# Features out of PSUM: one VectorE product per tile in place of two ScalarE copies, in a top-k attention with capacity-dropped experts

## The chip, the cores and the metric

One core of a Trainium2 chip runs the whole program. The metric is device time in microseconds (us) of one execution. The engines are called as in the profile: PE is TensorE (matmuls and transposes; PEld its weight loads), DVE is VectorE, ACT is ScalarE, POOL is GpSimd, SP is SyncE, whose queue issues most of the DMAs.

## What is computed

Eight sequences of 576 tokens with 8 heads of size 64 go through an attention that keeps, in each row, the scores not below the 32nd largest. The result, as 4608 tokens of 512 features, goes to a mixture of 8 experts, where each expert takes at most 80 of the tokens that choose it.

```python
scores = scale * np.matmul(q, k.transpose(0, 1, 3, 2))
kth = np.partition(scores, -top_k, axis=-1)[..., -top_k:-top_k + 1]
scores = np.where(scores >= kth, scores, -1000000000.0)
attn = np.exp(scores - np.max(scores, axis=-1, keepdims=True))
attn = attn / (np.sum(attn, axis=-1, keepdims=True) + 1e-09)
x = np.matmul(attn, v)                       # heads side by side: 4608 x 512
...
logits = x @ w_gate                          # one expert per token, 80 at most per expert
h = np.maximum(x[tok_idx] @ w1[e], 0.0)
out[tok_idx] = gate_w[tok_idx, None] * (h @ w2[e])
```

The change is in the division by the sum: the features `x` of a tile are what the product with `v` left in PSUM, times the reciprocal of the row's sum.

## The kernel before

**Tiles.** Attention works on pairs of heads: 8 sequences with 4 pairs each make 32 head pairs `n`. The 576 rows of a pair are cut into four full tiles of 128 rows (t = 0 to 3), each with both heads, and one tail tile of 64 rows (t = 4), in which the two heads lie on partitions 0 to 63 and 64 to 127. A unit is one head of one full tile, or the tail tile: 9 units a pair, 288 in all. `run` makes one step per unit, and the instructions of a step belong to several units at different stages.

**Stages of a unit.** `front` (PE, L226) makes the scores in the PSUM tile `sp`; ACT copies them, scaled, to `s` (L233). DVE takes the eight largest of each of six pieces (`cand`, L241), and from these searches the 24th largest in `search` (L252, L260). ACT then counts how many scores lie above it with a Sign pass (L257), POOL multiplies scores and signs to `y` (L263), DVE takes the eight next from `y` (L265), and a small DVE operation, the pick (L268), writes the threshold. `below` makes the mask from it: for odd units on ACT (L277), for even ones on POOL (L279). `turn_w` transposes scores and masks together on PE into PSUM (L315, L320; tiles `ab` and `cc`), ACT takes the exponential into `wT` (L322, L324), and `back` multiplies with `v` on PE (L335). Its result for head h stands in `cc` from column 256 + 65 h on: 64 features and, as 65th column, the sum of the weights.

**The division.** `over` lets DVE take the reciprocals of the sums, for both heads at once, into `z_all` (L347; the letter "z" in the order). `divide` then brings the features to `xn` in SBUF with one ACT copy per head (L358), whose scale is the column of reciprocals: 2 copies of 128x64 for a full tile, 2 of 64x64 for the tail tile. That frees `cc`, of which there are two.

**Behind it.** When a pair is complete, `norm` stores `xn` to the DRAM tensor `xd` with two DMAs on SP (L367, L369), transposes it on PE (L201), copies it on ACT (`xT`, L375), multiplies it with the gate weights (L380), and ACT copies the logits out (L387); for all but the first pair of a sequence DVE adds them up (L391). After every second sequence, `gates` works on the logits of two sequences together (L402 to L425). `turn` transposes the q and k of the next pair (L201) into `sp`, and ACT copies them as `both` (L214).

**What sets the order.** Everything in `run` is under a manual schedule: each engine executes its instructions in the order in which `step` issues them. In a step, a string of letters gives the order on DVE first; behind it come `turn_w`, `divide`, `front`, `back` and the `norm` pieces. "G" is one L241, "a" the last of these and the first L252, "b", "c", "d", "e", "y", "g" and "h" move the `search` of a unit one to four steps back on by one instruction each; "z" is the reciprocal, "m" and "M" are the masks. Because a pair has nine steps, its tiles end on odd steps in one pair and on even steps in the next, so that what surrounds "z" repeats every 18 steps.

```python
for c in "GybGcGdGeGGzag" if i % 2 else "GGbghHmMyGcGdGeGza":
...
if whole(i - 4):
    self.turn_w(*units[i - 4][:2])
for u in done:
    self.divide(*u)
```

After attention, `route` and `finish` choose the tokens and run the experts; the change doesn't touch them. A second, slower form of the whole program (`batch`, with `lean`) follows behind a condition that doesn't hold for these inputs.

Of the kernel before, what the change touches and what calls it, by code (L numbers as in the profile page):

```python
# [14 lines left out]
Act = mybir.ActivationFunctionType  # L15
Alu = mybir.AluOpType
# [11 lines left out]
def kernel(  # L28
# [11 lines left out]
    nc = tc.nc  # L40
    B, H, S, D = q.shape
# [7 lines left out]
    scale = 1.0 / math.sqrt(D)  # L49
    P = 128  # L50
    HP = H // 2
    NP = B * HP
    NF = S // P
    TL = S - NF * P
# [94 lines left out]
    class Attention:  # L149
# [199 lines left out]
        def divide(self, n, t):  # L349
            if t == 0:  # L350
                self.xn[n] = self.rows.tile([P, NK, 2, D], F32, name="xn", tag="xn")
            cc = self.w.pop((n, t))
            for h in range(2):
                if t < NF:
                    p, o, j, m = slice(0, P), 2 * P + h * (D + 1), h, P
                else:
                    p, o, j, m = slice(TL * h, TL * h + TL), 2 * P, 0, TL
                nc.scalar.activation(self.xn[n][:m, t, h, :], cc[p, o : o + D], Act.Copy, scale=self.z[p, n % NP, t, j : j + 1])  # L358

        def norm(self, n, b, hp, bi, nb, cs=range(NK)):  # L360

# [65 lines left out]
        def run(self, slow):  # L427

            units = []
            for n in range(NP):  # L430
                for t in range(NF):
                    units += [(n, t, 0), (n, t, 1)]
                units.append((n, NF, 2))
            self.odd = set(range(1, NU, 2))
            first, second = {}, {}
            later = []
            due = []
            drawn = []
            ready = {}

            def whole(i):

                return 0 <= i < NU and units[i][2] > 0

            def step(i, last):
                if 0 <= i < NU:
                    n, t, h = units[i]
                    if t == 2 and h == 1 and n + 2 < NP:
                        self.load(n + 2, *divmod(n + 2, HP))
                    if t in (1, 3) and h == 0 and slow and n:  # L450
                        slow.pop(0)()
                    if t == 0 and h == 0 and n + 1 < NP:
                        due.append(n + 1)
                    first[i] = self.parts(i)


                back = dict(a=0, b=1, c=1, d=1, e=1, y=2, g=3, h=4, m=4, H=3, M=3)
                for c in "GybGcGdGeGGzag" if i % 2 else "GGbghHmMyGcGdGeGza":
                    if c == "G":
                        if 0 <= i < NU:  # L460
                            next(first[i])
                    elif c == "a":
                        if 0 <= i < NU:
                            next(first[i], None)
                            second[i] = self.search(i)
                            next(second[i])
                    elif c == "z":
                        for u in drawn:
                            self.over(*u)
                    elif c in "mM":  # L470
                        if 0 <= i - back[c] < NU:
                            self.below(i - back[c])
                    elif i - back[c] in second:
                        next(second[i - back[c]])
                done = list(drawn)
                drawn.clear()

                def back():
                    if whole(i - 5):
                        self.back(*units[i - 5][:2])  # L480
                        drawn.append(units[i - 5][:2])


                rest = whole(i - 4) and units[i - 4][2] == 2
                if rest:
                    back()
                if whole(i - 4):
                    self.turn_w(*units[i - 4][:2])
                for u in done:
                    self.divide(*u)  # L490

                ends = [(n, range(NK) if n < NP - 1 else range(NF) if t < NF else range(NF, NK))
                        for n, t in done if t == NF or (n == NP - 1 and t == NF - 1)]

                f = i + 4 if i not in (0, 1) else i + 3
                busy = 0 <= f < NU and units[f][2] != 1
                if busy:
                    self.front(*units[f][:2])
                if not rest:
                    back()  # L500
                if due and not busy and i > 0:
                    self.turn(due.pop())
                    busy = True
                for g in list(later):
                    if ready[g] and busy and not last:
                        continue
                    busy = busy or ready[g] == 1
                    ready[g] = next(g, None)
                    if ready[g] is None:
                        later.remove(g)  # L510
                for n, cs in ends:
                    b, hp = divmod(n, HP)
                    later.append(self.norm(n, b, hp, b % 2, 2, cs))
                    ready[later[-1]] = 0

            with tc.manual_schedule():
                self.load(0, 0, 0)
                self.load(1, *divmod(1, HP))
                nc.sync.dma_start(wg, moe_w_gate.rearrange("(c p) e -> p c e", p=P))
                self.turn(0)  # L520
                i = -4
                while i < NU + 6 or later:
                    step(i, i >= NU + 5)
                    i += 1
            assert not slow and not due
# [389 lines left out]
```

## Time and profile before

Three runs took 994.33, 994.34 and 996.04 us; the median is 994.34. The profiled execution took 994.13 us, of which its span, from the first to the last instruction, is 992.4 us. The mean granted TensorE clock is 0.983.

| what | from the profile |
|---|---|
| profiled execution, its span | 994.13 us, 992.4 us |
| L358, the copies to `xn` on ACT | 320, busy 86.6 us, 324 ns (128x64) and 305 ns (64x64) |
| L347, the reciprocals on DVE | 160, busy 24.6 us, 152 ns (128x2) and 159 ns (128x1) |
| L241, the largest of six pieces, DVE | 1728, busy 400.6 us, 246 ns |
| L265, the largest of `y`, DVE | 288, busy 216.4 us, 752 ns; DVE idle before it 45.8 us, for POOL's `y` |
| L263, `y` on POOL | 288, busy 365.3 us, 1280 ns; POOL idle before it 65.9 us, for ACT's sign |
| L279, masks on POOL | 144, busy 247.9 us, 1722 ns; POOL idle before it 178.3 us, mostly for the pick |
| L335, product with `v`, PE | 5760, busy 205.2 us; PE idle before it 42.7 us, for `wT` |
| L391, sum of the logits on DVE, 128x40 | 23, 199 ns in the mean |

A group's line in the profile gives the number of instructions, how long their engine was busy with them, the mean duration of one, and how long the engine had stood idle just before them, with what ended the wait. Durations on one engine overlap: the next instruction often starts before the last one has ended, so the time between two starts, the step, is the price of an instruction in a full queue, and it is shorter than its duration. "L358 ACT xn<-cc,z_all" reads: line 358, on ACT, writes `xn` from `cc` and `z_all`.

### The profile page before, as it was taken

The page shows a single profiled execution, that of the slowest core. Times are in us where ns is not written, and L with a number is a line of the kernel's source. Part 1 is how long each engine was busy: PE and PEld are TensorE (multiplying, and loading weights), DVE is VectorE, ACT ScalarE, POOL GpSimd, SP SyncE. Part 2 cuts the span into 40 slices and gives each one's busy share as a digit, 9 for nine tenths or more (in the row PEclk, how much of TensorE's full clock was granted, in tenths as well). Part 3 has the DMA queues.
Part 4 walks back from the last instruction along what each step waited for, and adds up shares of the span by engine and source line. Part 5 has one row for each costly group of instructions (what it writes and reads, how often), then busy time and mean ns, then how long its engine had stood idle before and what let it go on. Part 6 is the DMA issues. An engine that isn't in the chain of part 4 may idle for free.

```text
span 992.4 us, 35679 instructions
## 1 busy us (share of the span) xinstructions
PE 881.3 (89%) x13368; PEld 710.3 (72%) x13368; DVE 804.6 (81%) x4928; ACT 798.2 (80%) x1652; POOL 627.3 (63%) x474
## 2 busy tenths in 40 slices
PE   5899999999989999999899999999899998689996
PEld 3677777777767777777677777777677776578896
DVE  5798989898989898999989898989898989471110
ACT  3899999999989999999899999999899999501110
POOL 3677767676767777777677676766677777402111
PEclk9999999999999999999999999999999999979999
DMA  3445453333323233333111122222222200084921
GB/s 72 102 123 133 126 135 91 92 92 92 93 76 77 75 87 86 88 90 92 46 41 44 44 50 50 51 50 49 49 50 50 50 13 14 16 339 147 368 85 29
DMA packets 167797, 85.76 MB, mean 86 GB/s; under 512 B 117696, under 2 KB 154560, under 8 KB 167616
## 3 DMA queue, kind: packets, MB, share of 16 engines
q1 hardware_dynamic: 166592, 80.78, 29.1%
q0 software_dynamic: 1024, 2.62, 0.9%
q8 instruction: 107, 1.75, 0.7%
q14 instruction: 74, 0.61, 0.2%
HBM read 63.19 MB, written 20.19 MB: 84 GB/s over the span
## 4 chain that ended last, share of the span: by engine, by line
DVE 46%; PE 26%; ACT 15%; POOL 7%; issue 5%; DMA 1%; POOLq 0%; SPq 0%; DVEq 0%; ACTq 0%
DVE cand L241 15%; DVE w L265 11%; DVE cand L260 6%; PE cc L335 5%; DVE top L252 5%; ACT sign L257 5%; POOL y L263 5%; PE sp L226 4%; PE yp L799 4%; DVE pick L268 3%; ACT wT L324 3%; ACT mask L277 3%; PE sp L201 2%; DVE w L252 2%; POOL mask L279 2%
## 5 line engine op out<-in xcount | busy, mean ns | idle before, releaser
L241 DVE MAX8 cand<-s 128x8 f32<-128x96 f32 x1728 | 400.6, 246 | 9.0 <-ACT s L233 8.8
L263 POOL TENSOR_TENSOR y<-s,sign 128x576 f32<-128x576 f32 x288 | 365.3, 1280 | 65.9 <-ACT sign L257 65.9
L279 POOL TENSOR_SCALAR mask<-s,thr_all 128x576 bf16<-128x576 f32 x144 | 247.9, 1722 | 178.3 <-DVE pick L268 175.4
L335 PEld LDWEIGHTS cc<-vb,wT 128*64 128x64 f32 x5760 | 182.8, 139 | 113.6 <-ACT wT L324 100.1
L265 DVE MAX8 w<-y 128x8 f32<-128x576 f32 x288 | 216.4, 752 | 45.8 <-POOL y L263 45.8
L335 PE MATMUL cc<-vb,wT 128*64 128x65 f32 x5760 | 205.2, 226 | 42.7 <-ACT wT L324 42.7
L257 ACT ACTIVATE sign<-s,w 128x576 bf16<-128x576 f32 x288 | 225.2, 782 | 7.1 <-POOL y L263 3.0
L226 PE MATMUL sp<-both 64*128 64x288 f32 (+1 forms) x1280 | 203.2, 437 | 17.5 <-ACT part L387 9.5
L233 ACT ACTIVATE s<-sp 128x1152 f32<-128x1152 f32 (+1 forms) x161 | 167.4, 1040 | 12.2 <-PE sp L226 9.9
L315 PE MATMUL ab<-ident,s 128*128 128x128 f32 x1148 | 176.2, 283 | 0.0
L324 ACT ACTIVATE wT<-ab 128x1024 f32<-128x1024 f32 (+1 forms) x159 | 149.1, 937 | 0.0
L226 PEld LDWEIGHTS sp<-both 64*128 64x128 f32 (+1 forms) x1280 | 106.1, 180 | 56.4 <-ACT part L387 11.4
L315 PEld LDWEIGHTS ab<-ident,s 128*128 128x128 f32 x1148 | 127.9, 142 | 11.6 <-issue 0.9
L252 DVE MAX8 top<-cand 128x8 f32<-128x48 f32 x576 | 116.0, 201 | 4.5
L277 ACT ACTIVATE mask<-s,thr_all 128x576 bf16<-128x576 f32 x144 | 112.4, 781 | 6.9 <-DVE pick L268 6.5
L320 PEld LDWEIGHTS <-mask 128*128 128x128 bf16 x1440 | 94.2, 98 | 31.9 <-POOL mask L279 29.2
L260 DVE MATCH_REPLACE8 cand<-top,cand 128x48 f32<-128x48 f32 x576 | 110.9, 193 | 0.0
L358 ACT ACTIVATE xn<-cc,z_all 128x64 f32<-128x64 f32 (+1 forms) x320 | 86.6, 320 | 1.2 <-DVE z_all L347 0.8
L315 PE MATMUL cc<-ident,s 128*128 128x128 f32 x288 | 79.1, 275 | 0.0
L322 ACT ACTIVATE wT<-cc 128x256 f32<-128x256 f32 (+1 forms) x160 | 56.9, 356 | 16.8 <-PE cc L320 15.5
L268 DVE SCALAR_TENSOR_TENSOR pick<-past,cnt,w 128x9 f32<-128x9 f32 x288 | 60.3, 223 | 0.3 <-ACT xn L358 0.3
L257 ACT ACTIVATION_READ_ACCUMULATOR sign<-s,w 128x1 f32 x288 | 58.7, 204 | 0.0
(187 smaller groups left out, 909.4 us busy)
## 6 DMA issues: line engine op xcount, KB each, us to landing
w<-in_moe_w_dram SPq DMA_DIRECT2D x10, 2048.0 KB, 11.6
w<-in_moe_w_dram SPq DMA_DIRECT2D x24, 512.0 KB, 4.6
out_dram<-zero SPq DMA_DIRECT2D x9, 1024.0 KB, 6.5
qn<-in_q_dram SPq DMA_DIRECT2D x64, 128.0 KB, 2.5
kn<-in_k_dram SPq DMA_DIRECT2D x64, 128.0 KB, 2.5
vb<-in_v_dram SPq DMA_DIRECT2D x64, 128.0 KB, 2.7
xd<-xn SPq DMA_DIRECT2D x32, 256.0 KB, 3.8
qn<-in_q_dram SPq DMA_DIRECT2D x32, 32.0 KB, 2.3
```

The source lines that it names most:

```text
L226: nc.tensor.matmul(o, lhsT=qT[d, t * P : t * P + m], rhs=kT[d, j * HS : (j + 1) * HS], start=True, stop=True)
L233: nc.scalar.activation(s[:, j * HS : (j + w) * HS].rearrange("p (j c) -> p j c", c=HS), ps[:, j : j + w, :HS], Act.Copy, scale=TINY)
L241: nc.vector.max(out=cand[:, j, :], in_=s[:, j * S // NG : (j + 1) * S // NG])
L252: nc.vector.max(out=dst, in_=cand)
L257: nc.scalar.activation(sign, s, Act.Sign, bias=w9[:, 7:8], scale=-1.0, accum_out=cnt)
L260: nc.vector.match_replace(out=cand, in_to_replace=dst, in_values=cand, imm_value=LOW)
L263: nc.gpsimd.tensor_tensor(out=y, in0=s, in1=sign, op=Alu.mult)
L265: nc.vector.max(out=w9[:, 8:], in_=y)
L279: nc.gpsimd.tensor_scalar(self.mask[i], self.s[i], self.thr[:, i : i + 1], None, op0=Alu.is_lt)
L315: nc.tensor.matmul(dst[h][c], lhsT=sc[:, keys[c]], rhs=ident, start=c == 0 or (c == NF and h == 0), stop=False, is_transpose=True, skip_gr ...
L324: nc.scalar.activation(wT[:, : g * NF, :], ab.rearrange("p h c r -> p (h c) r")[:, : g * NF, :], Act.Exp, scale=scale / TINY)
L335: nc.tensor.matmul(cc[r : r + TL, o], lhsT=wT[:, h * NF + c if c < NF else 2 * NF + h, r : r + TL], rhs=vb[:, c, h if t < NF else r // TL, ...
```

## The change

For a full tile, `divide` issues one DVE product of 128 x 2 x 64 elements: `cc` without its two columns of sums, times the two reciprocals broadcast over 64 columns. For the tail tile it issues two DVE products of 64x64, one a head; the second reads partitions 64 to 127 and writes partitions 0 to 63. ACT no longer takes part. In the order of a step the products have a letter of their own, "x": in odd steps it stands between "a" and "g" (behind the reciprocal and the first L252 of a new search, ahead of L265), in even steps at the end (so that the next step's first L241 follows). Before, the copies were issued behind `turn_w`.

```diff
             cc = self.w.pop((n, t))
+            o, xn, z = 2 * P, self.xn[n], self.z[:, n % NP, t, :].unsqueeze(2)
+            if t < NF:
+                nc.vector.tensor_tensor(out=xn[:, t, :, :], in0=cc[:, o : o + 2 * (D + 1)].rearrange("p (h d) -> p h d", h=2)[:, :, :D],
+                                        in1=z.to_broadcast([P, 2, D]), op=Alu.mult)
+                return
             for h in range(2):
-                if t < NF:
-                    p, o, j, m = slice(0, P), 2 * P + h * (D + 1), h, P
-                else:
-                    p, o, j, m = slice(TL * h, TL * h + TL), 2 * P, 0, TL
-                nc.scalar.activation(self.xn[n][:m, t, h, :], cc[p, o : o + D], Act.Copy, scale=self.z[p, n % NP, t, j : j + 1])
+                p = slice(TL * h, TL * h + TL)
+                nc.vector.tensor_tensor(out=xn[:TL, t, h, :], in0=cc[p, o : o + D], in1=z[p, 0, :].to_broadcast([TL, D]), op=Alu.mult)
...
-                for c in "GybGcGdGeGGzag" if i % 2 else "GGbghHmMyGcGdGeGza":
+                for c in "GybGcGdGeGGzaxg" if i % 2 else "GGbghHmMyGcGdGeGzax":
...
+                    elif c == "x":
+                        for u in drawn:
+                            self.divide(*u)
...
-                for u in done:
-                    self.divide(*u)
```

## The prediction

> **What bounds the kernel now.** I read the page's first part, then the windows of the attention stage, then the waits, then the timeline with the chain of waits. Attention (30 to 861 us) holds 84% of the span, and nothing after it is touched.
>
> ```profile
> PE 881.3 (89%) x13368; PEld 710.3 (72%) x13368; DVE 804.6 (81%) x4928; ACT 798.2 (80%) x1652; POOL 627.3 (63%) x474
> 548.75:600.46 51.71, 47.42 (x694) 37.62 (x694) 47.65 (x301) 48.85 (x102) 38.02 (x27) 1.00 0.22 51
> DVE w L265 <- POOL y L263: 3.7, 4, 1.2
> DVE z_all L347 <- PE cc L335: 1.3, 1, 1.3
> ```
>
> The second line is a window of 51.71 us: busy PE, PEld, DVE, ACT, POOL. It is two head pairs, nine steps each, and comes 16 times. ACT is busiest (48.85) and DVE next (47.65), so "whoever is fullest" says ACT bounds. The waits inside the window say otherwise: DVE stands still only 3.78 us, at four places (1.20 at 548.75, 1.29 at 553.97, 0.65 at 561.38, 0.64 at 577.97); for the rest the chain runs along DVE. So DVE sets the pace wherever it doesn't wait, and a removed ACT instruction pays only if it lies on the way to one of the four waits.
>
> Around the 0.64 the copies do lie on that way (ACT, then DVE):
>
> ```profile
> 573.63 0.52 ACT L358 ACTIVATE xn<-cc,z_all 128x64 f32<-128x64 f32 x2
> 574.03 1.15 ACT L233 ACTIVATE s<-sp 128x1152 f32<-128x1152 f32 x1
> 575.04 0.80 ACT L277 ACTIVATE mask<-s,thr_all 128x576 bf16<-128x576 f32 x1
> 575.71 0.79 ACT L257 ACTIVATE sign<-s,w 128x576 bf16<-128x576 f32 x1
> ...
> 577.97 0.76 DVE L265 MAX8 w<-y 128x8 f32<-128x576 f32 x1 [0.64 <-POOL y L263]
> ```
>
> Around the 1.20 they don't:
>
> ```profile
> 596.52 1.13 ACT L214 COPY both<-sp 128x1152 f32<-128x1152 f32 x1 [0.99 <-PE sp L201]
> 597.54 0.78 ACT L277 ACTIVATE mask<-s,thr_all 128x576 bf16<-128x576 f32 x1
> 598.22 0.77 ACT L257 ACTIVATE sign<-s,w 128x576 bf16<-128x576 f32 x1
> ...
> 600.46 0.76 DVE L265 MAX8 w<-y 128x8 f32<-128x576 f32 x1 [1.21 <-POOL y L263]
> ```
>
> Here ACT itself had stood 0.99 us for PE. That path goes from the second pick of DVE (584.18) by POOL's mask (584.38), PE, xT, mask, sign, exp, PE, "both" (596.52), to L265 and on by L322, L324 and PE's L335 to the z of 605.68: 21.5 us in which no copy of xn delays anyone.
>
> **The change part by part.** *Removed:* 320 ACT copies, 86.6 us busy. A pair moves ACT on by 0.40 us (573.63 to 574.03), by 0.65 in the tail tile (582.27 to 582.92).
>
> *Added:* 128 products of 128x128 and 64 of 64x64 on DVE. No row multiplies out of PSUM. What counts is the step to the next instruction, not the duration:
>
> ```profile
> 585.44 0.15 DVE L347 RECIPROCAL z_all<-cc 128x2 f32<-128x2 f32 x1
> 585.56 0.21 DVE L252 MAX8 top<-cand 128x8 f32<-128x48 f32 x1
> 585.69 0.24 DVE L241 MAX8 cand<-s 128x8 f32<-128x96 f32 x1
> 585.85 0.07 DVE L260 MATCH_VALUE_LOAD cand<-top,cand 128x8 f32 x1
> ...
> 872.40 0.46 DVE L681 FIND_INDEX8 ix<-top,cd_ps 128x8 uint32<-128x288 f32 x1
> 872.77 0.07 DVE L681 MATCH_VALUE_LOAD ix<-top,cd 128x8 f32 x1
> 872.83 0.45 DVE L681 FIND_INDEX8 ix<-top,cd 128x8 uint32<-128x288 f32 x1
> 873.20 0.07 DVE L681 MATCH_VALUE_LOAD ix<-top,cd 128x8 f32 x1
> ```
>
> 96 elements step 0.16 and 576 (L265) 0.66, so a step is about 0.06 plus 1.04 ns an element; L717, a product of 384 with a broadcast operand, steps 0.47 (887.42 to 887.89), the same line. From PSUM the step is no longer: 0.37 at 872.40 (from cd_ps) and 0.37 at 872.83. So 128 elements cost 0.20. Upper bound: a full duration, 0.15 fixed plus 0.13, 0.28. The product's wait for the reciprocal is free, since L252 stands between (0.24 from z's start, where z lasts 0.15).
>
> The two tail products: at least two steps of 64, 0.25. At most each is drained before the next starts: 0.15 + 0.07 + 0.03 = 0.245, twice 0.49 (L252 waiting for its L241 shows the 0.03 to 0.04: 587.06, 0.24 long, to 587.34). The second reads from partition 64 and writes to partition 0, which no DVE row here does, so I take the upper, 0.49.
>
> [...]
>
> *Moved:* the product comes at DVE's third place behind z, before "g" (L265) or the next step's L241; behind it in the queue stand the searches, the picks, and so POOL's masks and ACT's signs. ACT loses its wait for z (0.8 us, once). SP's two stores of xn now wait for DVE; they are issued in the same place, their data is there 1.5 to 2 us earlier, and SP's loads behind them gain rather than lose. PE's transposes into cc wait for the product of two tiles back, some 5 us old. All these at nothing; were the product late, PE's L315 would be late next.
>
> *Sum for one window,* each segment ending where it now waits:
> A, pick to z (the 21.5 above): the products fall into DVE's 2.5 us of waits (4 x 0.20 = 0.8) and cost nothing. PE's xn and qn transposes begin 0.12 late now behind ACT's s (589.21 and 594.84, against 1.31 after L335's start as elsewhere); both gaps go: -0.24.
> B, z (553.97) to L265 (561.38): ACT's way loses the 0.62 copy, but s then waits for PE's L226 (556.83): -0.43. DVE's way: the 0.65 wait goes, 0.49 + 0.20 come: +0.04. The later counts: +0.04.
> C, L265 to L265 (577.97): ACT's way -0.40. DVE's: -0.64, another -0.14 of small waits for POOL (566.69, 572.01), + 3 x 0.20: -0.18. The later: -0.18.
> D, to the pick (584.18), DVE all the way: one tail, +0.49.
> Total +0.11, times 16 = +1.8 us. At the end z (862.65), copies (862.85, 0.63 for two) and xT (863.51) are one chain; with the copies off ACT, xT needs only PE's transposes (end 863.12): -0.36. Together +1.4 on the profiled execution's 994.13 (span 992.4 and 1.7 around it), 0.2 under the median of 994.34: **996 us**.
>
> **The rivals.** *The small products overlap* (0.25 a tail): A -0.24, B -0.20, C -0.18, D +0.25 = -0.37 a window, -5.9 in all, with the end -6.3: 988. For it: three L425 products take 0.37 together. Against: those all start at partition 0.
>
> *Products at full duration* (0.28, 0.49): A -0.24, B +0.12, C +0.06, D +0.49 = +0.43, +6.9 in all: 1001. For it: it reads one operand from PSUM and one from SBUF, which no row does. Against: the 0.37 rows.
>
> *The product must wait for POOL* (the other side, slower). It has happened to products of two SBUF operands:
>
> ```profile
> 268.84 2.52 POOL L263 TENSOR_TENSOR y<-s,sign 128x576 f32<-128x576 f32 x2
> ...
> 268.92 1.29 DVE L412 TENSOR_TENSOR oh<-oh,mx 128x80 f32<-128x80 f32 x1
> ```
>
> 0.24 became 1.29, until POOL's first y ended; L391 likewise took 0.58 at 853.60 under a y ending 854.13. Under POOL's mask it took 0.18 (580.29, mask from 579.04 to 580.76). In the odd half the products would start at 565.47 and 570.79, as POOL's second y begins (565.40, 570.71): 1.19 each; the tail at 554.2 waits 0.47. B +0.51, C +2.20: +2.96 a window, +47: 1041. It decides from the moment in which one operand in SBUF is enough for the clash. Against: the other operand lies in PSUM. [...]
>
> *ACT was the bound* and all DVE waits go: 51.71 - 3.78 - 0.28 (four small waits like those in C) + 8 x 0.20 + 2 x 0.25 = 49.75, -31 in all: 963. For it: ACT's 48.85. Against: segment A, 21.5 us without a copy.
>
> That the product isn't issued where the diff says has no room: the order is written by hand, and in the built program's sequence for DVE it stands behind z and L252.
>
> **How the numbers follow.** Forecast 0.31, overlapping tails 0.27, full duration 0.23, waiting for POOL 0.13, ACT bound 0.06. The two outer cases, 0.19, stay outside; the inner three span 988 to 1001; some 4 us below and 9 above are added for small waits that shift (the products stand in front of every search, so the room is larger above): 984 to 1010. 0.2% is 2 us, about what a measurement here can tell from no change. Faster: 0.06 + 0.26 + 0.04 of the forecast's own spread = 0.36. Same: 0.13 of the forecast, 0.01 of the tails = 0.14. Slower: 0.14 + 0.23 + 0.13 = 0.50.
>
> **What would show it.** DVE busy some 45 us higher, ACT 87 lower, and the time hardly moved. The wait at 548.75 stays at 0.4 to 0.6, z's wait at about 1.1, those at 561 and 578 vanish; in total L265's 45.8 falls to about 15 and z's 27.3 to about 22. Rows of the product: 0.28 for the full one; its next instruction 0.20 later. Step right or wrong by itself: the start of the instruction behind the second tail product (0.49 or 0.25 after the first). Products of over 0.5 in odd pairs would prove the clash. The prediction falls if segment A shortens by more than 0.24: then a copy was on it after all.

## The result, and the profile after

The changed kernel takes 1027.2 us (median of four runs, 1026.44 to 1029.66), against 994.34 before: a ratio of 1.033, with a 95% interval of 1.031 to 1.036. The forecast was 996 us with a range of 984 to 1010. It was wrong by 31 us. The profiled execution's span is 1024.7 us, 32.3 more than before, and its mean granted TensorE clock is 0.967 instead of 0.983.

First the page's busy times, and the waits summed by engine and line (total us, times, longest):

```profile
PE 893.4 (87%) x13368; PEld 722.5 (71%) x13368; DVE 855.5 (83%) x5120; ACT 736.4 (72%) x1332; POOL 626.9 (61%) x474
```

```profile
PEld L320 <- POOL mask L279: 52.3, 42, 3.0
PE cc L320 <- POOL mask L279: 44.6, 27, 2.8
...
DVE z_all L347 <- PE cc L335: 25.8, 19, 5.5
DVE w L265 <- POOL y L263: 23.8, 26, 2.8
```

DVE did lose waits: L265's fell from 45.8 us to 23.8. But PE now waits 44.6 us for POOL's masks, against 23.1 before, and PE is 12 us busier with the same number of matmuls. The groups of DVE, separated by shape (busy us, mean ns, idle before), name the cause:

```profile
L355 DVE TENSOR_TENSOR xn<-cc,z_all 128x128 f32<-128x128 f32 x128 | 35.6, 278 | 0.1
L393 DVE TENSOR_TENSOR lg<-lg,part 128x40 f32<-128x40 f32 x23 | 20.2, 880 | 0.4
L360 DVE TENSOR_TENSOR xn<-cc,z_all 64x64 f32<-64x64 f32 x64 | 13.9, 217 | 0.6
```

The two kinds of product cost what was priced. The sum of the logits (L391 before, L393 now), which nobody touched, rose from 199 ns in the mean to 880. Its place before, in the timeline (start, duration, engine, line):

```profile
579.04 1.72 POOL L279 TENSOR_SCALAR mask<-s,thr_all 128x576 bf16<-128x576 f32 x1 [1.10 <-DVE pick L268]
...
580.04 0.15 DVE L347 RECIPROCAL z_all<-cc 128x1 f32<-128x1 f32 x1
580.16 0.21 DVE L252 MAX8 top<-cand 128x8 f32<-128x48 f32 x1
580.29 0.18 DVE L391 TENSOR_TENSOR lg<-lg,part 128x40 f32<-128x40 f32 x1
...
580.73 2.51 POOL L263 TENSOR_TENSOR y<-s,sign 128x576 f32<-128x576 f32 x2
...
586.16 0.23 PE L320 MATMUL cc<-minus,mask 128*128 128x128 bf16 x1 [0.82 <-POOL mask L279]
```

The same place after the change, and what comes of it:

```profile
595.37 1.73 POOL L279 TENSOR_SCALAR mask<-s,thr_all 128x576 bf16<-128x576 f32 x1 [1.20 <-DVE pick L268]
...
596.62 0.44 DVE L360 TENSOR_TENSOR xn<-cc,z_all 64x64 f32<-64x64 f32 x2
597.06 2.52 POOL L263 TENSOR_TENSOR y<-s,sign 128x576 f32<-128x576 f32 x2
597.09 1.31 DVE L393 TENSOR_TENSOR lg<-lg,part 128x40 f32<-128x40 f32 x1
...
598.32 0.25 DVE L241 MAX8 cand<-s 128x8 f32<-128x96 f32 x1
...
602.31 1.72 POOL L279 TENSOR_SCALAR mask<-s,thr_all 128x576 bf16<-128x576 f32 x1 [2.73 <-DVE pick L268]
...
604.09 0.23 PE L320 MATMUL cc<-minus,mask 128*128 128x128 bf16 x1 [2.41 <-POOL mask L279]
...
604.47 1.92 PE L226 MATMUL sp<-both 64*128 64x288 f32 x8
...
606.32 2.29 PE L335 MATMUL cc<-vb,wT 128*64 128x65 f32 x40
```

Read it from the top. Before, the sum started 0.44 us ahead of POOL's `y`, inside POOL's mask. The two tail products, 0.48 us, stand directly ahead of it and use up that margin: it now starts 0.03 us after `y` and ends when the first `y` does, after 1.31 us. The searches behind it are late, so is the pick, so is POOL's next mask (idle 2.73 us), and PE waits 2.41 us for it, where the same wait before was 0.82 (at 586.16). Then something new: the matmuls behind that wait are slow. L226 takes 1.92 us and L335 2.29, where they take 1.24 and 1.39 just before (at 597.54 and 598.77). The windows of two head pairs, from one such sum to the next (length; busy PE, PEld, DVE, ACT, POOL; granted clock; DMA share; GB/s), tell the two effects apart:

```profile
544.26:597.09 52.83, 47.25 (x691) 37.62 (x690) 50.83 (x313) 45.12 (x83) 38.01 (x29) 1.00 0.20 47
597.09:651.31 54.22, 48.60 (x691) 38.74 (x690) 50.92 (x311) 45.00 (x83) 38.00 (x29) 0.97 0.19 46
```

In the first window the clock stayed at 1.00: 52.83 against 51.71 before, +1.12, which is what the sum lost (1.31 - 0.18 = 1.13). In the second it fell to 0.97 and 1.39 us more were lost, nearly all on PE (48.60 busy against 47.25). The sum is late 14 times, in the second and fourth pair of the first seven sequences: 14 x 1.13 = 15.8 us (the expectations below count 15 times). Between 100 and 830 us PE's clock is halved (granted clock 0.50) for 12 periods of 3.41 us (11 stretches, one of them twice as long), against 2 before: 10 x 1.39 = 13.9 us. With the +1.4 that the forecast gave the rest this makes 31.1, of 32.9 measured. The rest has the size of what the stage behind attention grew: from the last sum to the end 127.9 us instead of 126.2.

### The profile page after: what moved, and what is told of

Its sections match the earlier page's. It is cut to its first block, busy times and chain, and to the rows that moved or that the text cites. A ratio compares the mean times of both kernels' runs of the same rounds, so it can differ in the third digit from the quotient of the medians.

```text
span 1024.7 us, 35457 instructions
## 1 busy us (share of the span) xinstructions
PE 893.4 (87%) x13368; PEld 722.5 (71%) x13368; DVE 855.5 (83%) x5120; ACT 736.4 (72%) x1332; POOL 626.9 (61%) x474
## 4 chain that ended last, share of the span: by engine, by line
DVE 61%; PE 23%; ACT 8%; issue 4%; POOL 3%; DMA 0%; POOLq 0%; DVEq 0%; ACTq 0%
DVE cand L241 18%; DVE w L265 14%; DVE cand L260 7%; DVE top L252 6%; PE cc L335 5%; DVE pick L268 4%; PE yp L802 4%; PE sp L226 4%; DVE w L252 3%; PE sp L201 2%; ACT wT L324 2%; ACT sign L257 2%; ACT mask L277 2%; DVE lg L393 2%; DVE xn L355 2%
## 5 line engine op out<-in xcount | busy, mean ns | idle before, releaser
L241 DVE MAX8 cand<-s 128x8 f32<-128x96 f32 x1728 | 400.0, 245 | 9.1 <-ACT s L233 9.0
L279 POOL TENSOR_SCALAR mask<-s,thr_all 128x576 bf16<-128x576 f32 x144 | 248.1, 1723 | 223.3 <-DVE pick L268 179.5
L335 PEld LDWEIGHTS cc<-vb,wT 128*64 128x64 f32 x5760 | 192.9, 145 | 117.7 <-ACT wT L324 103.5
L335 PE MATMUL cc<-vb,wT 128*64 128x65 f32 x5760 | 215.7, 232 | 45.4 <-ACT wT L324 45.4
L257 ACT ACTIVATE sign<-s,w 128x576 bf16<-128x576 f32 x288 | 222.0, 771 | 22.8 <-POOL y L263 16.7
L265 DVE MAX8 w<-y 128x8 f32<-128x576 f32 x288 | 216.1, 750 | 24.3 <-POOL y L263 23.8
L226 PE MATMUL sp<-both 64*128 64x288 f32 (+1 forms) x1280 | 206.1, 442 | 14.1 <-ACT part L389 6.1
L226 PEld LDWEIGHTS sp<-both 64*128 64x128 f32 (+1 forms) x1280 | 106.8, 181 | 53.5 <-ACT part L389 8.0
L320 PEld LDWEIGHTS <-mask 128*128 128x128 bf16 x1440 | 94.6, 98 | 54.2 <-POOL mask L279 52.3
L252 DVE MAX8 top<-cand 128x8 f32<-128x48 f32 x576 | 115.0, 200 | 4.5
L322 ACT ACTIVATE wT<-cc 128x256 f32<-128x256 f32 (+1 forms) x160 | 56.4, 352 | 32.3 <-PE cc L320 32.3
L320 PE MATMUL cc<-minus,mask 128*128 128x128 bf16 x144 | 32.2, 224 | 45.0 <-POOL mask L279 44.6
L320 PE MATMUL ab<-minus,mask 128*128 128x128 bf16 x576 | 56.3, 221 | 0.0
```

The source lines that it names most:

```text
L226: nc.tensor.matmul(o, lhsT=qT[d, t * P : t * P + m], rhs=kT[d, j * HS : (j + 1) * HS], start=True, stop=True)
L241: nc.vector.max(out=cand[:, j, :], in_=s[:, j * S // NG : (j + 1) * S // NG])
L252: nc.vector.max(out=dst, in_=cand)
L257: nc.scalar.activation(sign, s, Act.Sign, bias=w9[:, 7:8], scale=-1.0, accum_out=cnt)
L265: nc.vector.max(out=w9[:, 8:], in_=y)
L279: nc.gpsimd.tensor_scalar(self.mask[i], self.s[i], self.thr[:, i : i + 1], None, op0=Alu.is_lt)
```

## The experiments

The theory: the products are as cheap as forecast, and the tail products alone push one small sum under POOL's `y`; PE's clock then doubles the bill. The rivals: that a product itself costs more than its rows show (being held, or delaying L265), that the tail products are merely too long, or that all of it is lost to PE's clock for another reason.

**The sum two steps later.** The changed kernel, with one edit: for the second and fourth pair of a sequence the sum is issued two slots later in its steps, where it meets a POOL mask.

```diff
+            if hp % 2 and n < NP - 1:
+                yield 0
+                yield 0
             if hp > 0:
                 nc.vector.tensor_tensor(out=lg, in0=lg, in1=part, op=Alu.add)
```

> The changed kernel, but the sum of the logits (lg, L393 there) of the second and fourth pair of a sequence is issued two steps later, where POOL makes a mask and not y. Theory 'clash': the two tail products (0.48 us) pushed this sum under POOL's y, where it takes 1.31 in place of 0.18 us, the late pick lets PE stand 2.4 us for POOL's mask, and PE's clock then drops; nothing else was lost. It expects all lg sums at 0.18 but for one or two, no more half-speed stretches of PE in attention than the 3 of the kernel before, and about 996 us (994.1 plus the 1.4 of the prediction). Rival 'load': DVE has 41 us more to do (128 steps of 0.20 and 32 of 0.48) and pays for what its waits don't hold; without the clash only 15 x 1.13 = 17 us come back: 1010 us, with the clock still dropping.

Measured: 994.67 us (ratio to before 1.0003, 0.9989 to 1.0017). The whole loss is gone with all 160 tiles still on DVE. The sum and its neighbours in the timeline, and the window:

```profile
582.97 1.72 POOL L279 TENSOR_SCALAR mask<-s,thr_all 128x576 bf16<-128x576 f32 x1 [1.50 <-DVE pick L268]
...
584.50 0.19 DVE L396 TENSOR_TENSOR lg<-lg,part 128x40 f32<-128x40 f32 x1
584.66 2.52 POOL L263 TENSOR_TENSOR y<-s,sign 128x576 f32<-128x576 f32 x2
...
584.75 0.23 PE L320 MATMUL cc<-minus,mask 128*128 128x128 bf16 x1 [1.19 <-POOL mask L279]
```

```profile
428.27:480.00 51.73, 47.26 (x690) 37.62 (x690) 49.75 (x313) 45.26 (x82) 38.01 (x28) 1.00 0.28 72
```

The sum is back at 0.19, inside the mask. The windows without `gates` are 51.73 and 51.61 (376.66 to 428.27) in turn, +0.02 and -0.10 on before, where the segments of the forecast gave +0.11. It is not entirely clean: two of the moved sums near a change of rhythm still met a `y` (1.24 us at 322.18, 1.04 at 838.68), and the only two stretches of halved clock in attention (330.9 and 839.5) stand behind these two.

**Only the tail tiles on DVE,** the full ones left to ACT, and **only the full tiles on DVE,** the tails left to ACT, each in the order that the two kernels have for it:

```diff
 # only the tail tiles on DVE
+            if t < NF:
+                for h in range(2):
...
+                    nc.scalar.activation(self.xn[n][:m, t, h, :], cc[p, o : o + D], Act.Copy, scale=self.z[p, n % NP, t, j : j + 1])
+                return
...
                         for u in drawn:
-                            self.divide(*u)
+                            if u[1] == NF:
+                                self.divide(*u)
...
+                for u in done:
+                    if u[1] < NF:
+                        self.divide(*u)
 # only the full tiles on DVE
             for h in range(2):
-                p = slice(TL * h, TL * h + TL)
-                nc.vector.tensor_tensor(out=xn[:TL, t, h, :], in0=cc[p, o : o + D], in1=z[p, 0, :].to_broadcast([TL, D]), op=Alu.mult)
...
+                nc.scalar.activation(self.xn[n][:m, t, h, :], cc[p, o : o + D], Act.Copy, scale=self.z[p, n % NP, t, j : j + 1])
...
                         for u in drawn:
-                            self.divide(*u)
+                            if u[1] < NF:
+                                self.divide(*u)
...
+                for u in done:
+                    if u[1] == NF:
+                        self.divide(*u)
```

> The changed kernel with the full tiles back on ACT (two copies each behind turn_w, as before) and only the two tail products on DVE. Theory 'clash': everything that was lost comes by the tail products, so the loss stays: 15 sums at 1.31, some 10 to 14 half-speed stretches in attention, and 1020 to 1035 us, with only 32 x 0.48 = 15 us of work added to DVE. Rival 'load': at most 15 us more than before, 1000 to 1009 us.

> The other part alone: full tiles by one product on DVE, the tail tile by two ACT copies behind turn_w as before. Theory 'clash': the lg sum keeps its place under POOL's mask (0.18 us), the clock holds, and by the segments of the prediction a window changes by -0.24 (A), 0 (B, ACT's way keeps its copy), -0.18 (C), 0 (D) = -0.42, 16 times: 987 us, faster than both. Rival 'load': 128 x 0.20 = 26 us more on DVE, of which its waits hold a part: 1000 to 1015 us.

Measured: the tails alone 1028.11 us (1.0335, 1.0308 to 1.0361), the full tiles alone 991.78 (0.9978, 0.9966 to 0.999). With the tails alone the sum is late at the same 14 places (1.31 us at 13 of them, 1.15 at the other); with the full tiles alone it stays at 0.18. A window of each, the tails alone first:

```profile
600.26:654.66 54.40, 48.68 (x692) 38.43 (x690) 49.53 (x303) 48.17 (x99) 38.06 (x29) 0.97 0.19 46
```

```profile
417.03:468.20 51.17, 47.24 (x692) 37.61 (x691) 48.80 (x310) 45.98 (x86) 38.02 (x28) 1.00 0.33 90
```

So the 128 products of full tiles are a gain of 0.54 us a window, and the 64 small ones carry the whole loss. The gain in time with full tiles alone fell short of its expectation of 987: attention ended 5.8 us earlier (the last sum at 860.37, against 866.18), but the stage behind it took 129.3 us instead of 126.2. PE's clock does not explain that by itself: behind the last sum it is halved for 20.1 us, against 22.7 before.

**PE kept busy through its wait.** The changed kernel, with 24 matmuls of zeros put in front of the mask that comes late; they add zeros to columns 400 to 511 of `cc`, which nothing reads.

```diff
                 mk = self.mask.pop(i + h)
+                if t == 1 and n % 2 and h == 1 and not self.lean:
+                    for _ in range(24):
+                        nc.tensor.matmul(cc[:, 400:512], lhsT=zero.bitcast(BF16)[:, :P], rhs=zero.bitcast(BF16)[:, :112], start=False, stop=True, skip_group_check=True)
```

> The changed kernel with 24 matmuls of zeros (128x112, bf16, into unused columns of cc) put on PE where it waits 2.4 us for POOL's mask (second tile of every other pair, ahead of that mask's products). The clash of the lg sum stays, the idle stretch of PE is filled. If the dropping clock costs the other half of the loss: half-speed stretches in attention fall from 17 to 5 or fewer, the lg sums stay at 1.31, and the time is about 1011 us (17 us over before). If the clock only goes along with the loss and costs nothing itself: 1027 us as in the changed kernel. If the fillers are longer than the wait they cost: more than 1027.

Measured: 1015.51 us (1.0214, 1.0192 to 1.0235). The timeline shows the late mask unchanged, the added matmuls in the gap, and normal speed behind it:

```profile
590.52 1.31 DVE L396 TENSOR_TENSOR lg<-lg,part 128x40 f32<-128x40 f32 x1
...
594.95 1.34 PE L321 MATMUL cc<-zero 128*128 128x112 bf16 x24
595.74 1.72 POOL L279 TENSOR_SCALAR mask<-s,thr_all 128x576 bf16<-128x576 f32 x1 [2.73 <-DVE pick L268]
...
597.52 0.23 PE L323 MATMUL cc<-minus,mask 128*128 128x128 bf16 x1 [1.23 <-POOL mask L279]
...
597.90 1.24 PE L226 MATMUL sp<-both 64*128 64x288 f32 x8
599.14 1.39 PE L338 MATMUL cc<-vb,wT 128*64 128x65 f32 x40
```

```profile
590.52:643.26 52.74, 48.45 (x715) 38.81 (x714) 50.84 (x311) 45.16 (x83) 37.99 (x29) 1.00 0.20 47
```

The sum still takes 1.2 to 1.3 us 14 times, but PE works through 1.34 us of a wait that had been 2.4, the clock stays at 1.00, and 11.7 of the 32.9 us are gone (1027.2 - 1015.5). The stretches of half clock between 100 and 830 us number 2, as before the change (the 17 of the expectation are those of the whole execution; in these 730 us there had been 11). The expectation of 1011 was missed by 4.5. Of this, 2.9 us lie behind attention (129.1 us from the last sum to the end, 126.2 before). One window that holds the `gates` operations is 2.5 us longer than before (696.11 to 752.70, where it was 683.72 to 737.77): the sum explains 1.13 of it, and the rest has the size of the stretch of halved clock that this window has at 710.9 and before had none of.

**The clash alone, without the change.** In the kernel before, the sum of the same pairs is put off by four DVE instructions, so that it starts where `y` starts. The copies stay on ACT, and the eighth sequence is included, so there are 15 places.

```diff
-            if hp > 0:
+            if hp % 2 and n < NP - 1 and not self.lean:
+                self.owed.append(lambda: nc.vector.tensor_tensor(out=lg, in0=lg, in1=part, op=Alu.add))
+            elif hp > 0:
...
-                for c in "GybGcGdGeGGzag" if i % 2 else "GGbghHmMyGcGdGeGza":
+                for c in "GybGlcGdGeGGzag" if i % 2 else "GGbghHmMyGcGdGeGza":
...
+                    elif c == "l":
+                        while self.owed:
+                            self.owed.pop()()
```

> The kernel before, copies on ACT and no product, in which only the sum of the logits of the second and fourth pair is issued four DVE instructions later (behind the second piece of the next step, 0.6 us later), when POOL's y has begun. DVE has nothing more to do. Theory 'clash': 15 sums take about 1.2 in place of 0.18, PE waits for the mask, its clock drops some ten times: 1015 to 1030 us, nearly the time of the changed kernel without any of the change. Rival 'load': what counts is the work that was added to DVE and not this sum: 994 to 997 us.

Measured: 1021.24 us (1.0247, 1.0199 to 1.0295; four runs from 1012.55 to 1022.18), with no product on DVE at all. The timeline at one of the 15 places, and two windows:

```profile
592.70 1.72 POOL L280 TENSOR_SCALAR mask<-s,thr_all 128x576 bf16<-128x576 f32 x1 [1.10 <-DVE pick L269]
...
594.39 2.51 POOL L264 TENSOR_TENSOR y<-s,sign 128x576 f32<-128x576 f32 x2
594.44 1.28 DVE L392 TENSOR_TENSOR lg<-lg,part 128x40 f32<-128x40 f32 x1
...
595.64 0.20 DVE L253 MAX8 top<-cand 128x8 f32<-128x48 f32 x1
```

```profile
432.95:485.76 52.81, 47.41 (x691) 37.61 (x690) 48.76 (x301) 49.07 (x103) 38.02 (x28) 1.00 0.32 87
594.44:648.66 54.22, 48.81 (x691) 38.74 (x690) 48.68 (x300) 49.19 (x103) 38.07 (x28) 0.97 0.19 46
```

The same two lengths as after the change, 52.8 at full clock and 54.2 with one drop, and the same order of loss (27 us). All 15 sums take 1.27 to 1.29 us, and between 100 and 830 us there are 11 stretches of halved clock. So the moved sum makes a loss of this size by itself, whoever does the division.

**The other products of two SBUF operands.** The kernel before has three more such clashes: the comparison `oh` of `gates` (L412) takes 1.29 us in three of its four places. In three kernels it is issued two slots later:

```diff
             nc.vector.tensor_reduce(mx, oh, axis=AX, op=Alu.max)
+            if not self.lean and b0 < B - nb:
+                yield 0
+                yield 0
             nc.vector.tensor_tensor(out=oh, in0=oh, in1=mx.unsqueeze(2).to_broadcast([P, GM, E]), op=Alu.is_equal)
```

In the kernel before:

> The kernel before with nothing changed but the comparison of the gates two steps later, as in the run of the full tiles. There it took 1.29 us three times. Theory 'clash': 3 x 1.05 us and up to two clock stretches (the windows around 290 and 500 us show a clock of 0.97): 988 to 992 us. Rival: 994, no change.

In the kernel with only the full tiles on DVE:

> The kernel with full tiles on DVE and tail tiles on ACT, and the comparison of the gates (oh, 128x80, two operands in SBUF) issued two steps later in the first three groups, where POOL makes a mask and not y. In that kernel it takes 1.09, 1.09 and 0.95 us against 0.24. Theory 'clash': each of the three is worth 0.8 to 0.85 us on DVE's path, and where PE stood still behind it also the 1.4 to 1.6 us of a clock stretch: 2.5 to 7 us less, 985 to 989 us. Rival: the place of that sum has slack behind it: 990 to 992, no change.

In the kernel with all tiles on DVE and the sum two steps later:

> The changed kernel with all products on DVE and both sums out of POOL's way: the logits' sum of the second and fourth pair and the gates' comparison two steps later. Theory 'clash': what the change itself is worth without any clash is this run against the kernel before with the gates' comparison moved (987.2): by the windows' sum +0.02 to +0.11 us each, so 986 to 990 us; and it stays behind the run with full tiles alone on DVE (982.3) by the tail products' 16 x 0.5. Rival 'load': 41 us more on DVE show once the clashes are gone: above 992.

Measured: 987.17 us (0.9938, 0.9922 to 0.9955), 982.29 (0.9878, 0.9861 to 0.9894) and 990.91 (0.9979, 0.9966 to 0.9993). Two of the three came out below their expectations (988 to 992 and 985 to 989), the last just above (986 to 990). Three clashes that had been in the kernel all along were worth 7 us; with them the two stretches of halved clock between 100 and 830 us are gone too. With full tiles on DVE, tails on ACT and none of these clashes the kernel takes 982.3 us, the best of all measured here. Its groups by shape:

```profile
L396 DVE TENSOR_TENSOR lg<-lg,part 128x40 f32<-128x40 f32 x23 | 4.6, 199 | 0.0
L420 DVE TENSOR_TENSOR oh<-oh,mx 128x80 f32<-128x80 f32 x4 | 0.9, 234 | 0.0
```

The change as it was made, freed of its clash, costs 3.7 us against the kernel before freed of its own (990.9 against 987.2); two clashes are left in it (`oh` 0.90 us at 695.93, the sum 1.30 at 834.32). A part of these 3.7 us doesn't lie in attention at all: in the seven profiles with products on DVE the stretch from the last sum to the end takes 127.9 to 129.5 us, in the three with all copies on ACT 125.6 to 126.2, though the change doesn't touch its code. Why is open. Tails on DVE instead of ACT cost 8.6 us (990.9 against 982.3), those two clashes included. The windows shown above say the same: 51.73 with the tails and 51.17 without, a difference of 0.56, of which their own step of 0.48 is most.

## Why the prediction was wrong, point by point

**What bounds the kernel: right.** DVE sets the pace where it doesn't wait. The full tiles' products filled waits and small gaps and gained 0.54 us a window. The rival "ACT was the bound" had asked for 31 us of gain; the kernel with all products on DVE and both sums out of the way has ACT emptier by 59 us (738.9, against 797.9 in the kernel before with `oh` moved) and is 3.7 us slower.

**The price of the products: right, both terms.** Two places of the changed kernel's timeline, a tail in the odd half and a full tile under POOL's `y`:

```profile
570.77 0.46 DVE L360 TENSOR_TENSOR xn<-cc,z_all 64x64 f32<-64x64 f32 x2
571.25 0.76 DVE L265 MAX8 w<-y 128x8 f32<-128x576 f32 x1
...
580.80 2.53 POOL L263 TENSOR_TENSOR y<-s,sign 128x576 f32<-128x576 f32 x2
...
582.13 0.27 DVE L355 TENSOR_TENSOR xn<-cc,z_all 128x128 f32<-128x128 f32 x1
582.32 0.75 DVE L265 MAX8 w<-y 128x8 f32<-128x576 f32 x1
```

The pair of tail products steps 0.48 (0.49 forecast), the full one 0.19 (0.20 forecast) with 0.27 of duration. The rivals of overlapping tails and of full durations fall with these two numbers.

**"The product must wait for POOL": the wrong instruction.** At 582.13 the full product lies under `y` and takes its 0.27, so for this product one operand in SBUF was not enough for the clash, as the forecast argued. But the clash did decide the time. The case had named everything: L412 with 1.29 us under `y`, L391 with 0.58 under a `y`, L391 with 0.18 under the mask at 580.29. It asked only whether the *new* instruction would clash, and not whether the new instruction would push one of the *old* ones, which it had in hand, from the mask into `y`.

**The step that failed: segment D, "DVE all the way: one tail, +0.49", and the list under "Moved".** That list names as queued behind the product "the searches, the picks, and so POOL's masks and ACT's signs". The sum of the logits, which stands two places behind the reciprocal of a tail in the even half, is missing. Its margin was in the page of before: start 580.29, `y` at 580.73, 0.44 us. The forecast put 0.49 ahead of it. With the sum counted, segment D is +0.49 + 1.13 = +1.62, and 14 such windows give 996 + 16 = 1012, near the 1015.5 of the kernel whose PE was kept busy.

The starts of the same instructions after the change (z at 517.85, L265 at 525.22 and 541.50, pick at 549.28, z at 570.56, then 578.05, 594.32, 602.11 and 624.90) and in the kernel with the sum two steps later (552.44, 559.92, 576.19, 582.76, 604.16) measure the forecast segment by segment, in us against before:

| segment | before | forecast | after, clock full | after, clock drops | sum two steps later |
|---|---|---|---|---|---|
| A | 21.50 | -0.24 | -0.22 | +1.29 | -0.10 |
| B | 7.41 | +0.04 | -0.04 | +0.08 | +0.07 |
| C | 16.59 | -0.18 | -0.31 | -0.32 | -0.32 |
| D | 6.21 | +0.49 | +1.57 | +1.58 | +0.36 |

D alone is far off, and A where PE's clock drops behind the late mask. (In the last column the sum stands in A and no longer in D.)

**The second half, PE's clock, was in no case.** The forecast priced a late pick by DVE's own time. It did not ask how long PE would stand, though the trace of before had it: the windows from 262.62 and from 473.18, each with an `oh` under `y`, show waits of PE of 2.10 us and clocks of 0.97. (A third such wait, at 697.56, was followed by no drop.)

**The other parts.** The sum of A, B, C and D, +0.11, came out near nothing in the kernel with the sum two steps later (+0.01 in the table); A and B are as forecast within 0.14, and C gained 0.14 more than forecast, by waits that were not traced. There L265's wait falls to 13.1 us (15 forecast) and z's to 20.3 (22 forecast); the waits of 561 and 578 are gone, the one of 548.75 is 0.46, and z's 1.10. DVE's busy time rises by 36.1 us there, not 45, and ACT's falls by 62 after the change, not 87: the 87 is the whole busy time of the copies (86.6), part of which ran beside the neighbouring instructions (573.63 with 0.52, and the next at 574.03); how the 45 was made up, the forecast doesn't say.

## What to carry to other kernels

Before an instruction goes into a full in-order queue, list what stands behind it and look at each for a clash that it now misses by a margin; the margin (here 0.44 us) is read from the timeline, and it is compared with the step of what goes in (0.48). Work of one engine that is only slow beside certain work of another (here the sum, 0.18 us beside POOL's mask and 1.31 beside `y`) has a good and a bad slot, and moving it by two slots was worth more here (32.5 us, 1027.2 to 994.7) than anything the change could have given. When a wait of PE grows (here from 0.82 to 2.41 us), ask what its clock does afterwards (here 0.50 for 3.41 us).

## What the hardware showed that was not expected

**Beside which POOL work the DVE sum of two SBUF operands is slow.** Under POOL's product `y` (two operands) the sum lasts until the running `y` ends: 1.28 to 1.32 us where it starts with the `y`, which takes 1.28, and less where it starts later in one (0.58 at 853.60 before, under a `y` that runs from 852.85 to 854.13). Under POOL's mask (L279, one tensor operand, also from SBUF) it takes 0.18 at 580.29 before and 0.19 at 584.50 with the sum two steps later. What sets the mask apart (its one operand, or its bf16 output) no run tested.

**Behind PE's waits of 1.9 to 2.8 us its clock fell to 0.50 in most places, but not in all.** Behind the wait that ended at 604.09 the clock, in slices of half a microsecond, is 0.90 at 604.5, 0.50 from 605.0 to 608.0, and 1.00 again from 608.5. At 11 of the 14 waits of 2.40 us and more for a mask such a stretch began within 1.7 us of the wait's end; at those that ended at 169.50, 442.55 and 551.26 none did. In the kernel with the clash alone 11 waits were only 1.90 to 1.91 us long, and 8 of them were followed by one.

Waits of equal length differ in the traces by where they lie. In each of the ten profiles all stretches of halved clock begin on one grid of 3.41 us: before, those at 276.82, 488.45 and 843.43 are 62 and 104 such periods apart, after, those at 116.80, 222.62 and 280.64 are 31 and 17. The wait that ended at 604.09 lies within one window of that grid; the one that ended at 551.26 is cut by a border, 1.43 us on one side and 0.98 on the other:

```profile
601.49:604.91 3.42, 1.01 (x13) 0.69 (x12) 3.39 (x25) 2.20 (x5) 2.60 (x2) 1.00 0.00 0
604.91:608.32 3.41, 3.41 (x44) 2.52 (x42) 3.38 (x20) 2.58 (x4) 2.10 (x3) 0.50 0.00 0
546.87:550.29 3.42, 1.99 (x32) 1.73 (x27) 3.38 (x20) 1.82 (x4) 0.81 (x1) 1.00 0.16 43
550.29:553.70 3.41, 2.44 (x41) 1.79 (x43) 3.35 (x22) 2.91 (x6) 3.40 (x3) 1.00 0.00 0
```

(Windows again; the second column is the length, the third PE's busy time, the third from the end the clock.) From 60 to 850 us PE was busy for less than 0.48 of the time in 3 windows of the grid before and in 11 after, and each of the 14 was followed by one at 0.50. The next busier ones had 0.63 before and 0.55 after; from there on none was, apart from the one from 222.62, itself at 0.50, in a stretch that lasted two windows. Counted over the ten profiles, all 44 windows under 0.483 were followed by a halved one, between 0.483 and 0.55 it was 1 of 8, above that none, apart from 5 stretches that lasted two windows. In the two windows shown above, with the drop and without, it cost 1.39 us (54.22 against 52.83).
